# Preloaded late rows put in column order blocks ahead, the last scatter repeated behind the join, the flag read at step nine of every late block

## The chip, the cores and the metric

The kernel runs on one core of a Trainium2 chip. The metric is the device time of one execution in microseconds. PE is TensorE (matmuls), DVE is VectorE, ACT is ScalarE, POOL is GpSimd, SP is SyncE, which here only issues DMAs. PEld is PE's weight load, which runs beside its matmuls. A q behind an engine's name (PEq, POOLq) is its sequencer.

## The reference: what is computed

Three layers stand one behind the other. Eight batches of 3072 positions with 256 values pass a layer in the frequency domain, then 24576 tokens a two-layer network of width 2048, then a mixture of eight experts with room for 768 tokens each:

```python
X = rfft(x, axis=1)
Yr, Yi = Xr @ w_r - Xi @ w_i + b_r, Xr @ w_i + Xi @ w_r + b_i
Y = sign(.) * max(abs(.) - 0.01, 0)             # both parts
x = irfft(Y, n=3072, axis=1).reshape(24576, 256)

h = max(x @ w_in, 0); x = (h * h) @ w_out       # 256 -> 2048 -> 256

logits = x @ w_gate; e = argmax(logits)
# token i, in order: kept while its expert has fewer than 768 tokens so far
disp[e, counts[e]] = x[i]; pos[i] = counts[e]; counts[e] += 1
y = max(disp @ w1, 0) @ w2                      # per expert, 256 -> 1024 -> 256
out[i] = prob[i, e] * y[e, pos[i]]  if kept, else 0
```

Tokens that come after their expert is full give zeros. With this data all eight experts are full after about two thirds of the tokens.

## The kernel before

**Blocks and steps.** The 24576 tokens are worked in 48 blocks of 512, six to a batch; `b, o = divmod(i, 6)`. A block has 16 steps f; step f makes 128 of the 2048 hidden values (`l1`, six matmuls on PE, three products that split the number into a high and a low part). Blocks 0 to 10 are full: `l2` follows in each step, and `route` sends their rows into `disp`, the experts' input. Blocks from 11 on are *late*: from the hidden values only the gate's logits are made (`l2_gate`, at step 10 for the first half and at step 2 of the next block for the rest), since most of their tokens find their expert full. `route(i - 1)` then works beside block i, as a list of small operations (`rops`), of which so many are issued per step: 8 where `steps` is empty, else 5. `steps` are the operations of the next batch's FFT; they are empty at o = 0, o = 1 and, from about step 7, at o = 5.

**What route does in a late block.** DVE finds the chosen expert of each token (`oh`), PE counts by a prefix product with a triangular matrix (`prefix`, L652 and L654), DVE makes the places `pos`, the mask of the kept tokens `kp`, the new counts, the `flag` (some expert still has room), a second prefix product over `kp` gives each kept token's rank (`lp`, `li`). Four scatters on POOL (L667, `late<-zm,li`) write the weight, the token's number and its slot into the table `late`, by rank. `lcnt` and `nlate` count the late rows.

**The nested branches.** From block 12 on each block has one step, FX, at which all remaining small operations are issued and every engine reads the flag (L1227) and branches; the rest of the program stands inside that branch. FX is 9, or 7 (`FX_BARE`) where `steps` is empty. When no expert has room any more, the program leaves through the Else of that block to a common join. In this data it leaves at block 31 (b = 5, o = 1). In an Else (L1144) each engine only brings its semaphores to where the other way would have brought them; POOL waits there for its scatters.

**Behind the join.** The kept late tokens are computed again, with the whole network, in chunks of 256 rows: `late_rows` loads 256 entries of `late` (SP) and gathers the rows by token number from the DRAM array `yr` (POOL, two gathers); `row_order` copies them into column order (by halves of the 256 columns instead of bands of 32); `redo_y` transposes them on PE and splits them; `redo` runs the 16 steps and scatters into `disp`. Chunk c + 1 is loaded at step 4 of chunk c, put in order at step 5 and transposed at step 13. Seven chunks run here. The first chunk's rows, `row0`, are loaded and gathered already in step 1 of every block with o = 0 from block 12 on (12, 18, 24, 30), but put in order behind the join, one half by DVE and one by POOL. There SP also loads the first expert's weights (`m2_loadw(0)`, two loads of 1 MB) ahead of chunk 1's rows. The experts' phase follows.

**Transposes of the block's own rows.** At step 8 (`y_rows`) DVE turns the block's input rows and SP writes them to `yr`. At o = 5, step 9, the FFT stage's loads `xc<-z` are issued by SP, and PE uses them in the steps behind it (L417).

The lists are worked in this order within a step: `l1`, the scatters (`moves`, up to four a step), the small operations, `row0`, `y_rows`, the FFT, the flag.

Of the kernel before, what the change touches and what calls it, by code (L numbers as in the profile page):

```python
# [8 lines left out]
F32 = mybir.dt.float32  # L9
F32R = mybir.dt.float32r  # L10
BF16 = mybir.dt.bfloat16
I32 = mybir.dt.int32
# [7 lines left out]
P = 128  # L20
# [7 lines left out]
def fft_mix__moe__moe2_kernel(  # L28
# [20 lines left out]
    nc = tc.nc  # L49
    NB, S, D = x.shape  # L50
# [11 lines left out]
    TPB = BLK // P  # L62
    MW = 3
# [5 lines left out]
    RB = min(BLK, 256)  # L69
    NREDO = -(-NSLOT // RB)  # L70
    NSURE = max(NFULL + 1, -(-NSLOT // BLK))
# [22 lines left out]
    LG_WAIT = 0  # L94
    LG_T = 4
    PER_F = 5
    PER_BARE = 8
    FX_BARE = 7
    WARM = 16
    Y_F = 8  # L100
    assert E <= CG and KF == 2 * GQ and GQ % 4 == 0 and FX < GF
# [11 lines left out]
    yr = dram1.tile([NTOK, D], F32, name="yr")  # L113

    idt = keep.tile([P, P], F32, name="idt")
    zero = keep.tile([P, D], F32, name="zero")

    f1 = big.tile([N1, N1], F32, name="f1")
    gm = big.tile([N1, N1], F32, name="gm")
# [16 lines left out]

    flag = big.tile([P, 1], I32, name="flag")
    npre = big.tile([P, 1], I32, name="npre")

    class Fft:  # L140
        pass
# [467 lines left out]
    def by_half(ap):  # L609
        return ap.rearrange("p (k b c) -> p k b c", k=2, c=Q)  # L610

    def by_band(ap):
        return ap.rearrange("p (b k c) -> p k b c", k=2, c=Q)
# [49 lines left out]
    def scatter(dst, n, idx, zt, later=None, tiles=TPB):  # L663
# [15 lines left out]
        for t in range(tiles):  # L679
            if later is None:  # L680
                one_tile(t)
            else:
                later.append(lambda t=t: one_tile(t))

    def route(i, zt, lg, lt):
        v = nc.vector
        ops = []
# [65 lines left out]
        if lt is not None:  # L753
            lp = small([TPB + 1], F32, "lp")
            lx = small([TPB], F32, "lx")
            li = W.li()

            def ranks():
                pv = prefix(kp5.unsqueeze(2), 1)
                v.tensor_scalar(lp, pv[:, :, 0], lcnt, None, op0=ALU.add)  # L760

            ops.append(ranks)
            op(
                v.scalar_tensor_tensor,
                lx, lp[:, 0:TPB], -float(BIG), kp5[:, 0:TPB], op0=ALU.add, op1=ALU.mult,
            )
            op(v.tensor_scalar, li, lx, float(BIG), None, op0=ALU.add)
            last.append(lambda: v.tensor_copy(lcnt, lp[:, TPB:]))
            last.append(lambda: v.tensor_copy(nlate, lp[:, TPB:]))  # L769
            dst, n, idx = late, NREDO * RB, lambda t: li[:, t:t + 1]  # L770
        else:
            dst, n, idx = disp, NSLOT, lambda t: zt[:, t, D + 2:D + 3]
# [88 lines left out]
                oob_is_err=False,  # L861
            )

    def row_order(lt, rows, engs=(gp, gp)):
        for t in range(RB // P):
            engs[t % 2].tensor_copy(by_half(lt[:, t * D:(t + 1) * D]), by_band(rows[:, t, 0:D]))
        return lt

    def buf_init():
# [17 lines left out]
    def zero_fill():  # L887
        return [
            lambda r=r, buf=buf: nc.sync.dma_start(
                out=buf[r:r + ZR, :].rearrange("(p k) d -> p k d", p=P),  # L890
                in_=zero.unsqueeze(1).to_broadcast([P, ZR // P, D]),
            )
            for buf in (yr, out) for r in range(0, NTOK, ZR)
        ]
# [86 lines left out]
    with tc.manual_schedule():  # L981
# [150 lines left out]

        def go_on(value):
            guard = tc.If(value)
            ifs.append((guard, guard.__enter__()))

        def warm(p):
            for _ in range(WARM):
                nc.tensor.matmul(p[:, 0:D], idt, zero)

        def close_ifs(other=None):
            while ifs:
                guard, here = ifs.pop()
                guard.__exit__(None, None, None)  # L1144
                if other:
                    with here.Else():
                        other()

        for i in range(NBLK):
            b, o = divmod(i, BPB)  # L1150
# [22 lines left out]
            for f in range(KF):  # L1173
                hook = None
                if i + 1 < NBLK:
                    if f == (KF - 3 if o + 1 < BPB else KF - 1):
                        split_y(i + 1, 0)
                    if f == KF - 1:
                        hook = lambda i=i: split_y(i + 1, 1)
                q.append(l1(ys[i], f, not full, hook=hook, bare=not steps))  # L1180
                if i == 0 and f < 3:
                    combine_w(f)
                if f == CARRY and carry:
                    l2_gate(acc, GQ, carry)
                    pend = evac_gate(acc, *pend)
                if f == (CARRY if carry else 1) and pend is not None:
                    rops = route(i - 1, *pend)
                for _ in range(1 if full else MV):
                    if moves:
                        moves.pop(0)()  # L1190
                for _ in range(3 if full else PER_F if steps else PER_BARE):
                    if rops:
                        step = rops.pop(0)
                        if step is None:
                            break
                        step()
                if f == 1 and o == 0 and i >= NSURE:
                    nc.gpsimd.tensor_copy(npre, nlate)
                    late_rows(0, row0)

                if not full and f == Y_F:
                    y_out = y_rows(i)
                if y_out and f > Y_F:
                    y_out.pop(0)()
                if full and f >= 2:
                    l2(acc, f - 2, q)
                if f not in SKIP[full] or o == BPB - 1:
                    fft_share(1)
                if o == BPB - 1 and b + 1 < NB:
                    if f == SB_F:  # L1210
                        fft(1000)
                        for c in range(3):
                            load_z(st, c)
                        last = sb_steps(st)
                    if f >= KF - 1 - len(SB_N) and f < KF - 1:
                        for _ in range(SB_N[f - KF + 1]):
                            last.pop(0)()
                if not full and f == GF:
                    l2_gate(acc, 0, q)
                if f == (FX if steps else FX_BARE) and i >= NSURE:  # L1220
                    while moves or rops:
                        step = (moves or rops).pop(0)
                        if step is not None:
                            step()
                    if pair[0]:
                        fft(1)
                    rv = nc.values_load(flag[0:1, 0:1], min_val=0, max_val=1)  # L1227
                    go_on(rv > 0)
                if i < NSURE:
                    left = KF * (min(NSURE, NFULL, NBLK) - i) - f  # L1230
                    for k, n in ((0, KF - f), (1, left)):
                        for _ in range(-(-len(fill[k]) // max(n, 1))):
                            fill[k].pop(0)()
# [17 lines left out]
        while moves or rops:  # L1251
            step = (moves or rops).pop(0)
            if step is not None:
                step()
        close_ifs()
        spare.update({0: [], 1: []})
        CT = cap // P
        KD = F2 // P
# [15 lines left out]
        if NBLK > NFULL:  # L1274
# [44 lines left out]
                scatter(disp, NSLOT, lambda t: rows[:, t, D + 2:D + 3], rows, tiles=RT)  # L1319
                return (nxt, y_nxt) if ahead else None  # L1320

            nxt = row0, redo_y(row_order(W.lt(), row0, (ve, gp)))
            nv = nc.values_load(nlate[0:1, 0:1], min_val=0, max_val=NREDO * RB)
            n0 = nc.values_load(npre[0:1, 0:1], min_val=0, max_val=NREDO * RB)
            w_t[0] = m2_loadw(0)
# [220 lines left out]
```

## Time and profile before

| | |
|---|---|
| median of 3 runs | 2073.98 us (2072.65 to 2074.11) |
| the profiled execution | 2076.15 us, span 2074.4 us |
| mean granted clock of PE | 0.983 |
| PE busy | 1996.4 us (96%) |
| DVE, ACT, POOL busy | 1112.8 (54%), 1029.1 (50%), 465.9 us (22%) |
| POOL's scatters `late<-zm,li` | 80, 83.9 us, 1049 ns each |
| DMA | 231.06 MB, mean 111 GB/s |

The shares are of the span. Of the 40 slices of the span PE is busy 9 tenths or more in all but three: the first, the one with the join of the branches (from 1608 us) and the one with the start of the experts' phase (from 1763 us). The granted clock is below 9 tenths of full speed in the same three.

### The profile page before, as it was taken

What the parts mean: (1) busy time and instruction counts of PE and PEld (TensorE: products, weight loads), DVE (VectorE), ACT (ScalarE), POOL (GpSimd) and SP (SyncE); (2) the same over time, 40 slices, a digit from 0 to 9 for tenths busy, and PEclk for the clock granted to TensorE, in tenths of its full rate; (3) what the DMA queues carried; (4) which work ended last, traced back from release to release, by engine and by line L of the source; (5) the groups of instructions that cost most, each with busy time, mean ns of one, the idle gap of its engine ahead of it and who ended that gap; (6) DMA issues with size and microseconds to landing.
All of it is one profiled execution on the core that took longest, in us unless ns stands there. A gap on an engine that the chain in (4) does not pass through costs nothing. (4 is left out here: it accounts for less than half of the span.)

```text
span 2074.4 us, 33524 instructions
## 1 busy us (share of the span) xinstructions
PE 1996.4 (96%) x12577; PEld 1699.4 (82%) x12577; DVE 1112.8 (54%) x2378; ACT 1029.1 (50%) x2051; POOL 465.9 (22%) x495
## 2 busy tenths in 40 slices
PE   6999999999999999999999999999999699799999
PEld 3878999998899898667776687767777699799999
DVE  4846676664566774426634366334653466545352
ACT  3654444444444444566545665466554355424241
POOL 3730111110011111102211122201221122145442
PEclk8999999999999999999999999999999899899999
DMA  8769765567511113162332532333332100643400
GB/s 264 227 193 160 233 208 168 193 202 218 168 31 53 52 37 92 21 166 71 85 93 45 149 84 79 87 83 109 101 88 55 49 27 22 155 120 95 123 16 31
DMA packets 254271, 231.06 MB, mean 111 GB/s; under 512 B 97695, under 2 KB 230544, under 8 KB 254082
## 3 DMA queue, kind: packets, MB, share of 16 engines
q1 hardware_dynamic: 238322, 188.14, 33.0%
q0 software_dynamic: 10384, 21.63, 3.3%
q10 hardware_dynamic: 5376, 18.88, 2.6%
q8 instruction: 105, 1.72, 0.3%
q14 instruction: 84, 0.69, 0.1%
HBM read 111.40 MB, written 118.85 MB: 111 GB/s over the span
## 5 line engine op out<-in xcount | busy, mean ns | idle before, releaser
L549 PE MATMUL ph<-yh,wi_s 128*128 128x512 f32 (+1 forms) x1776 | 499.8, 403 | 6.3 <-DVE sf L691 3.7
L549 PEld LDWEIGHTS ph<-yh,wi_s 128*128 128x128 f32 x1776 | 311.3, 190 | 93.6 <-issue 21.7
L580 PE MATMUL acc<-wo_s,sh 128*128 128x264 f32 (+1 forms) x1792 | 337.4, 284 | 0.0
L580 PEld LDWEIGHTS acc<-wo_s,sh 128*128 128x128 f32 x1792 | 286.8, 188 | 13.6
L571 DVE TENSOR_TENSOR s<-s 128x512 f32<-128x512 f32 (+1 forms) x272 | 170.5, 627 | 202.0 <-ACT sh L570 195.8
L549 PE MATMUL ph<-yl,wi_s 128*128 128x512 f32 (+1 forms) x888 | 269.5, 385 | 0.2
L580 PE MATMUL acc<-wo_s,sl 128*128 128x264 f32 (+1 forms) x896 | 254.7, 284 | 1.0 <-DVE sl L572 1.0
L386 POOL TENSOR_TENSOR xc<-ue 64x256 f32<-64x256 f32 x120 | 101.0, 842 | 636.3 <-DVE ue L381 420.0
L567 ACT ACTIVATE s<-ph 128x512 f32<-128x512 f32 (+1 forms) x224 | 123.0, 549 | 229.5 <-PE ph L549 225.9
L560 ACT ACTIVATE ls<-ph 128x512 f32<-128x512 f32 x220 | 130.7, 594 | 175.2 <-PE ph L549 164.5
L549 PEld LDWEIGHTS ph<-yl,wi_s 128*128 128x128 f32 x888 | 163.1, 189 | 34.9 <-DVE yl L538 1.5
L572 DVE TENSOR_TENSOR sl<-s,sh 128x512 fp32r<-128x512 f32 (+1 forms) x272 | 163.0, 599 | 20.6 <-PE acc L549 0.5
L580 PEld LDWEIGHTS acc<-wo_s,sl 128*128 128x128 f32 x896 | 168.6, 188 | 1.9 <-DVE sl L572 1.9
L549 PE MATMUL acc<-yh,wi_s 128*128 128x512 f32 (+1 forms) x624 | 158.6, 376 | 2.2 <-DVE sf L691 1.9
L564 ACT ACTIVATE ls<-ls 128x512 f32<-128x512 f32 x248 | 156.6, 631 | 7.8
L667 POOL DMA_INDIRECT late<-zm,li x80 | 83.9, 1049 | 320.1 <-DVE nlate L769 131.6
L570 ACT ACTIVATE sh<-s 128x512 fp32r<-128x512 f32 (+1 forms) x272 | 151.4, 557 | 8.7
L1438 ACT ACTIVATE rh<-pg 128x384 fp32r<-128x384 f32 x128 | 62.6, 489 | 161.3 <-PE pg L1429 161.3
L1453 PE MATMUL po<-w2s,rh 128*128 128x256 f32 x768 | 138.5, 283 | 0.0
L1429 PE MATMUL pg<-xh,w1s 128*128 128x384 f32 x512 | 133.5, 339 | 3.6 <-issue 3.0
L549 PEld LDWEIGHTS acc<-yh,wi_s 128*128 128x128 f32 x624 | 104.8, 190 | 31.1 <-issue 8.5
L562 DVE TENSOR_TENSOR ls<-ls 128x512 f32<-128x512 f32 x80 | 55.4, 693 | 129.8 <-ACT ls L560 118.7
(301 smaller groups left out, 3430.2 us busy)
## 6 DMA issues: line engine op xcount, KB each, us to landing
yr<-zero SPq DMA_DIRECT2D x48, 512.0 KB
out_dram<-zero SPq DMA_DIRECT2D x48, 512.0 KB
uj<-u SPq DMA_DIRECT2D x72, 256.0 KB
z<-ue SPq DMA_DIRECT2D x72, 256.0 KB
xc<-z SPq DMA_DIRECT2D x46, 384.0 KB
u<-ue ACTq DMA_DIRECT2D x43, 384.0 KB
xc<-in_x_dram SPq DMA_DIRECT2D x35, 384.0 KB
yr<-zt SPq DMA_DIRECT2D x80, 128.0 KB
```

Of the source, the lines that this page charges most:

```text
L386: y_eng[n == r].tensor_tensor(y[64 * r:64 * r + 64, :], t[src, r, :], c[src, r, :], op=ALU.subtract)
L549: nc.tensor.matmul(p, wi_s[:, l, k, f * P:(f + 1) * P], y[:, k, 0:n_tok], start=(n == 0), stop=(n == 5),)
L560: nc.scalar.activation(s, p, AF.Relu)
L564: nc.scalar.activation(s, s, AF.Square)
L567: nc.scalar.activation(s, p, AF.Relu)
L570: nc.scalar.activation(sh, s, AF.Square)
L571: nc.vector.tensor_tensor(s, s, s, op=ALU.mult)
L572: nc.vector.tensor_tensor(sl, s, sh.bitcast(F32), op=ALU.subtract)
L580: nc.tensor.matmul(acc[t][:, 0:width], a[:, t * P:(t + 1) * P], wo_s[:, m, f, 0:width], start=(f == 0 and n == 0), stop=(f == KF - 1 and n ...
L667: inst = nc.gpsimd.indirect_dma_start(out=dst[:, :], out_offset=bass.IndirectOffsetOnAxis(ap=idx(t).bitcast(U32), axis=0), in_=zt[:, t, :] ...
L1429: nc.tensor.matmul(p[:, 0:gs], w1s[:, l, k, f * P:(f + 1) * P], y[:, k, g * gs:(g + 1) * gs], start=(n == 0), stop=(n == 5),)
L1453: nc.tensor.matmul(acc, a[:, t * P:(t + 1) * P], w2s[:, m, f, :], start=(n == 0), stop=(n == 3 * KD - 1),)
```

## The change

Five things are edited. (1) `PER_BARE` and `FX_BARE` go: five small operations a step and the flag at step 9 in every late block. (2) `row_order(zero, row0)` follows the gathers of `row0` in step 1 of the blocks 12, 18, 24 and 30, both halves on POOL; it writes into `zero`, a tile which is widened from 256 to 512 columns and whose zeros are needed only at the program's start. Behind the join `redo_y(zero)` transposes from there. (3) At the flag only `rops` is emptied, no longer `moves`. (4) Each Else, and the end of the last block, copies the last block's indices and entries (`li`, `zm`) to `lif` and `zmf` with three DVE copies (`hold`). (5) Behind the join four scatters write `zmf` by `lif` into `late`.

```diff
--- before.py
+++ after.py
@@ -94,8 +94,6 @@
     LG_WAIT = 0
     LG_T = 4
     PER_F = 5
-    PER_BARE = 8
-    FX_BARE = 7
     WARM = 16
     Y_F = 8
     assert E <= CG and KF == 2 * GQ and GQ % 4 == 0 and FX < GF
@@ -113,7 +111,7 @@
     yr = dram1.tile([NTOK, D], F32, name="yr")
 
     idt = keep.tile([P, P], F32, name="idt")
-    zero = keep.tile([P, D], F32, name="zero")
+    zero = keep.tile([P, RB // P * D], F32, name="zero")
 
     f1 = big.tile([N1, N1], F32, name="f1")
     gm = big.tile([N1, N1], F32, name="gm")
@@ -136,6 +134,8 @@
 
     flag = big.tile([P, 1], I32, name="flag")
     npre = big.tile([P, 1], I32, name="npre")
+    lif = big.tile([P, TPB], I32, name="lif")
+    zmf = big.tile([P, TPB, MW], F32, name="zmf")
 
     class Fft:
         pass
@@ -682,6 +682,8 @@
             else:
                 later.append(lambda t=t: one_tile(t))
 
+    held = []
+
     def route(i, zt, lg, lt):
         v = nc.vector
         ops = []
@@ -754,6 +756,7 @@
             lp = small([TPB + 1], F32, "lp")
             lx = small([TPB], F32, "lx")
             li = W.li()
+            held[:] = [li, zt]
 
             def ranks():
                 pv = prefix(kp5.unsqueeze(2), 1)
@@ -861,9 +864,9 @@
                 oob_is_err=False,
             )
 
-    def row_order(lt, rows, engs=(gp, gp)):
+    def row_order(lt, rows):
         for t in range(RB // P):
-            engs[t % 2].tensor_copy(by_half(lt[:, t * D:(t + 1) * D]), by_band(rows[:, t, 0:D]))
+            nc.gpsimd.tensor_copy(by_half(lt[:, t * D:(t + 1) * D]), by_band(rows[:, t, 0:D]))
         return lt
 
     def buf_init():
@@ -888,7 +891,7 @@
         return [
             lambda r=r, buf=buf: nc.sync.dma_start(
                 out=buf[r:r + ZR, :].rearrange("(p k) d -> p k d", p=P),
-                in_=zero.unsqueeze(1).to_broadcast([P, ZR // P, D]),
+                in_=zero[:, 0:D].unsqueeze(1).to_broadcast([P, ZR // P, D]),
             )
             for buf in (yr, out) for r in range(0, NTOK, ZR)
         ]
@@ -1132,19 +1135,25 @@
 
         def go_on(value):
             guard = tc.If(value)
-            ifs.append((guard, guard.__enter__()))
+            ifs.append((guard, guard.__enter__(), list(held)))
 
         def warm(p):
             for _ in range(WARM):
-                nc.tensor.matmul(p[:, 0:D], idt, zero)
+                nc.tensor.matmul(p[:, 0:D], idt, zero[:, 0:D])
 
         def close_ifs(other=None):
             while ifs:
-                guard, here = ifs.pop()
+                guard, here, block = ifs.pop()
                 guard.__exit__(None, None, None)
                 if other:
                     with here.Else():
-                        other()
+                        other(block)
+
+        def hold(block):
+            li, zm = block
+            nc.vector.tensor_copy(lif, li)
+            nc.vector.tensor_copy(zmf[:, :, 0:1], zm[:, :, 0:1])
+            nc.vector.tensor_copy(zmf[:, :, 1:].bitcast(I32), zm[:, :, 1:].bitcast(I32))
 
         for i in range(NBLK):
             b, o = divmod(i, BPB)
@@ -1188,7 +1197,7 @@
                 for _ in range(1 if full else MV):
                     if moves:
                         moves.pop(0)()
-                for _ in range(3 if full else PER_F if steps else PER_BARE):
+                for _ in range(3 if full else PER_F):
                     if rops:
                         step = rops.pop(0)
                         if step is None:
@@ -1197,6 +1206,7 @@
                 if f == 1 and o == 0 and i >= NSURE:
                     nc.gpsimd.tensor_copy(npre, nlate)
                     late_rows(0, row0)
+                    row_order(zero, row0)
 
                 if not full and f == Y_F:
                     y_out = y_rows(i)
@@ -1217,9 +1227,9 @@
                             last.pop(0)()
                 if not full and f == GF:
                     l2_gate(acc, 0, q)
-                if f == (FX if steps else FX_BARE) and i >= NSURE:
-                    while moves or rops:
-                        step = (moves or rops).pop(0)
+                if f == FX and i >= NSURE:
+                    while rops:
+                        step = rops.pop(0)
                         if step is not None:
                             step()
                     if pair[0]:
@@ -1252,7 +1262,9 @@
             step = (moves or rops).pop(0)
             if step is not None:
                 step()
-        close_ifs()
+        hold(held)
+        close_ifs(hold)
+        scatter(late, NREDO * RB, lambda t: lif[:, t:t + 1], zmf)
         spare.update({0: [], 1: []})
         CT = cap // P
         KD = F2 // P
@@ -1319,7 +1331,7 @@
                 scatter(disp, NSLOT, lambda t: rows[:, t, D + 2:D + 3], rows, tiles=RT)
                 return (nxt, y_nxt) if ahead else None
 
-            nxt = row0, redo_y(row_order(W.lt(), row0, (ve, gp)))
+            nxt = row0, redo_y(zero)
             nv = nc.values_load(nlate[0:1, 0:1], min_val=0, max_val=NREDO * RB)
             n0 = nc.values_load(npre[0:1, 0:1], min_val=0, max_val=NREDO * RB)
             w_t[0] = m2_loadw(0)
```

What stands on POOL in the last two blocks that run, 30 and 31, before (`row_1535` is `row0`, `zm` and `li` the entries and indices of a block's late rows):

```order
L1198 COPY npre<-nlate 128x1
L853 DMA row_1535<-yr,row_1535 128x256 x2
L691 IOTA zm_1528 128x4
L667 DMA late<-zm_1528,li_1533 6144x3 x4
L1227 TENSOR_LOAD flag
L1144 COMPARE_AND_BRANCH
L691 IOTA zm_1529 128x4
L667 DMA late<-zm_1529,li_1534 6144x3 x4
L1227 TENSOR_LOAD flag
L1144 COMPARE_AND_BRANCH
```

And the same place of the changed kernel (`row_1537` is `row0`):

```order
L1207 COPY npre<-nlate 128x1
L856 DMA row_1537<-yr,row_1537 128x256 x2
L869 COPY zero<-row_1537 128x256 x2
L693 IOTA zm_1530 128x4
L667 DMA late<-zm_1530,li_1535 6144x3 x4
L1237 TENSOR_LOAD flag
L1147 COMPARE_AND_BRANCH
L693 IOTA zm_1531 128x4
L667 DMA late<-zm_1531,li_1536 6144x3 x4
L1237 TENSOR_LOAD flag
L1147 COMPARE_AND_BRANCH
```

The two copies into `zero` have come behind the gathers of block 30. The four scatters of each block stand ahead of its flag read, as before: the scatters are among the moves that are issued at the start of step 9.

POOL at the join before, up to the end of chunk 0 (`zt_1527` holds the rows of chunk 1):

```order
L1144 UNCONDITIONAL_BRANCH
L866 COPY lt_1532<-row_1535 128x256
L1323 TENSOR_LOAD nlate
L1324 TENSOR_LOAD npre
L1144 COMPARE_AND_BRANCH
L853 DMA zt_1527<-yr,zt_1527 128x256 x2
L866 COPY lt_1532<-zt_1527 128x256 x2
L667 DMA disp<-row_1535 6144x259 x2
```

And in the changed kernel:

```order
L1147 UNCONDITIONAL_BRANCH
L667 DMA late<-zmf,lif 6144x3 x4
L1335 TENSOR_LOAD nlate
L1336 TENSOR_LOAD npre
L1147 COMPARE_AND_BRANCH
L856 DMA zt_1529<-yr,zt_1529 128x256 x2
L869 COPY lt_1534<-zt_1529 128x256 x2
L667 DMA disp<-row_1537 6144x259 x2
```

The copy has gone, and in its place four scatters stand ahead of the gathers of chunk 1.

DVE at the end of block 31's routing before (`ls` is the gate's hidden values, `zt` the transposed rows of the block):

```order
L691 TENSOR_SCALAR li_1534<-lx 128x4
L768 COPY lcnt<-lp 128x1
L769 CAST nlate<-lp 128x1
L562 TENSOR_TENSOR ls_8138<-ls_8138 128x512
L1227 TENSOR_LOAD flag
L1144 COMPARE_AND_BRANCH
L623 STREAM_TRANSPOSE zt_1526<-yT 128x1024
```

And in the changed kernel:

```order
L693 TENSOR_SCALAR li_1536<-lx 128x4
L771 COPY lcnt<-lp 128x1
L623 STREAM_TRANSPOSE zt_1528<-yT 128x1024
L562 TENSOR_TENSOR ls_8142<-ls_8142 128x512
L772 CAST nlate<-lp 128x1
L1237 TENSOR_LOAD flag
L1147 COMPARE_AND_BRANCH
```

The transpose now precedes the flag read, and SP's first write of the transposed rows to `yr` with it.

## Rows read from the trace of the kernel before

**Rows 1.** Waits of PE, 780 to 1616 us: total, times, longest.
```profile
PE ph L549 <- DVE sf L691: 3.7, 2, 1.9
PE acc L652 <- DVE kp L691: 1.4, 4, 0.3
PE acc L417 <- DMA xc<-z: 0.6, 1, 0.6
```

**Rows 2.** Chain of waits, 1600 to 1660 us: start, duration, what.
```profile
1599.91 1.41 PE ph L549 x6
...
1625.96 5.79 issue
1632.29 0.41 POOL lt L866
...
1633.89 1.66 PE ph L549 x6
```

**Rows 3.** Timeline at the exit, the join and chunk 1: start, us, engine, [idle before].
```profile
1616.70 1.48 POOL L667 DMA_INDIRECT late<-zm,li  x1 [22.21 <-DVE nlate L769]
...
1621.07 0.98 POOL L667 DMA_INDIRECT late<-zm,li  x1 [0.30 <-issue]
...
1623.44 1.19 SPq L1270 DMA_DIRECT2D yT<-in_moe_w_dram  x1
...
1626.54 0.45 PE L1295 MATMUL px<-idt,lt 128*128 128x128 f32 x1 [10.58 <-DVE lt L866]
...
1634.28 1.06 POOL L853 DMA_INDIRECT zt<-yr,zt  x1 [1.59 <-DVE yl L478]
...
1638.63 0.40 POOL L866 COPY lt<-zt 128x256 f32<-128x256 f32 x1 [0.89 <-DMA zt<-yr,zt]
...
1653.01 0.60 PE L1295 MATMUL px<-idt,lt 128*128 128x128 f32 x4
```

**Rows 4.** Instructions of line 1144 around the exit: ns min/median/max, first and last start.
```profile
L1144 POOLq EVENT_SEMAPHORE  x6: 17/30/43, 1622.2 to 1622.7; - x6
L1144 PEldq COMPARE_BRANCH  x2: 3085/3293/3501, 1615.1 to 1619.0; - x2
...
L1144 DVEq EVENT_SEMAPHORE  x2: 21/21/21, 1620.0 to 1620.1; - x2
...
L1144 POOLq INC_SWDGE_SEM  x1: 1050/1050/1050, 1624.8 to 1624.8; - x1
L1144 POOLq COMPARE_BRANCH  x1: 46/46/46, 1625.9 to 1625.9; - x1
```

**Rows 5.** Instructions of line 409, blocks 17 and 23.
```profile
L409 SPq EVENT_SEMAPHORE  x4: 17/28/28, 1053.0 to 1058.0; - x4
...
L409 SPq EVENT_SEMAPHORE  x4: 17/22/28, 1300.1 to 1304.7; - x4
```

**Rows 6.** Timeline of blocks 17 and 23, DVE and PE.
```profile
1051.37 1.25 DVE L623 STREAM_TRANSPOSE zt<-yT 128x1024 f32<-128x1024 f32 x1 [0.37 <-issue]
...
1059.45 0.80 PE L417 MATMUL acc<-gm,xc 96*128 96x96 f32 x6
...
1305.06 0.69 PE L417 MATMUL px<-gm,xc 96*128 96x96 f32 x5
```

**Rows 7.** Stretches: us, busy by engine PE to POOL, PEclk, DMA share, GB/s.
```profile
1633.90:1638.50 4.60, 4.60 (x22) 4.60 (x23) 2.21 (x6) 2.12 (x6) 2.48 (x3) 0.51 0.20 57
...
1781.00:1786.00 5.00, 5.00 (x14) 4.09 (x15) 0.00 (x0) 0.42 (x1) 0.00 (x0) 0.58 0.02 7
...
1051.30:1054.70 3.40, 3.40 (x10) 2.63 (x9) 1.25 (x1) 1.23 (x2) 2.11 (x3) 0.50 0.31 57
```

**Rows 8.** Timeline of a later chunk's rows: load, first gather, second copy.
```profile
1687.01 0.36 SPq L848 DMA_DIRECT2D zt<-late  x1
...
1689.50 1.05 POOL L853 DMA_INDIRECT zt<-yr,zt  x1 [4.25 <-DMA zt<-late]
...
1694.68 0.61 POOL L866 COPY lt<-zt 128x256 f32<-128x256 f32 x1 [1.71 <-DMA zt<-yr,zt]
```

## The prediction

> **What bounds the kernel now.** I read the table of PE's waits first, over the stretch of the late blocks, then the chain of waits around the join, then the timeline there, then the clock by stretches. PE is the bound nearly everywhere, so what the change can be worth is the sum of PE's gaps that it touches; work on other engines beside a busy PE costs nothing. The waits show three kinds of gap in the late blocks. Three times PE stops 1.9 us for the flag read that stands behind step 7, in blocks 17, 23 and 29 (the row on ph holds two of them; the third, of the same size, fell on acc). Eight times it stops 0.35 us for the kept mask (1.4 us on acc for four, and four more of that size on px): the blocks 12, 13, 18, 19, 24, 25, 30 and 31. Once, in block 29, it waits 0.6 us for an FFT load [rows 1]. The largest gap lies behind the exit of block 31. The reader is to see there that PE is idle 10.58 us to its first transpose at 1626.54, and that it then waits again, because POOL's copy of the second half of the preloaded rows starts at 1632.29 only, after 5.79 us of "issue"; step 0 of the first late chunk starts at 1633.89 [rows 2, 3]. The instructions of the branches say why POOL comes last: it has waited for its scatters (the semaphore instruction at 1624.8, 1.05 us), branches at 1625.9 and then shows nothing until 1631.75. Two branches of PE took 3.1 and 3.5 us [rows 4].
>
> **Flag back to step nine, five operations a step.** Blocks 14 to 16, 20 to 22 and 26 to 28 already work so and show no such gap, so I remove the gaps of the others. *Mask:* seven blocks other than 31 lose 0.35 us each: −2.45. *Blocks 17, 23, 29:* 3 x 1.85 = 5.6 us of gap go, but next in line is the load xc<-z. Its landing is the last event of line 409, 1058.0 in block 17 and 1304.7 in block 23 [rows 5]; PE used it at 1059.45 and 1305.06 [rows 6], and in block 29 right as it landed, since it waited for it [rows 1]. The load stands on SP behind the first write of the transposed rows, and that behind DVE's transpose, which now comes ahead of the branch; by its 0.37 us of idle there and 0.07 for the one small operation passed, it starts about 0.45 us earlier [rows 6]. So the gaps can shrink by 1.85 (1.45 + 0.45 covers it), 0.36 + 0.45 = 0.8, and 0.45: −3.1. What remains is a gap in front of the FFT stage, and gaps can cost clock: after the 1.85 us gap in block 17 the granted clock was 0.50 (the lower of the two levels) over 3.4 us, which costs 1.7 [rows 7]. I take 0.8 back for one half of such a drop: −2.3. Bounds: 0 (all given back), and −5.6 − 1.7 = −7.3 with the drop in block 17 gone and every load early.
>
> **Row order ahead of the join.** Two POOL copies of 0.40 us [rows 3] and the wait for the two gathers are added to blocks 12, 18, 24 and 30. Behind them on POOL stand the iota and the four scatters of that block, which nobody waits for on PE; POOL is idle over 20 us before such scatters (22.21) [rows 3]. Cost 0; if that cover were gone, 0.8 us a block plus the gathers' landing. The DVE copy and the POOL copy behind the join go.
>
> **The exit.** The changed kernel leaves two steps later and without the mask's gap: 2 x 1.41 − 0.35 = +2.47 [rows 1, 2]. POOL's Else began at 1622.2 [rows 4]; now at about 1624.7, and this is the last thing that PE needs for its transposes, since these read rows put in order long ago. From the copy's start at 1632.29 over three transposes and the split to step 0 it was 1.6 [rows 2]; the copy's 0.41 goes and a fourth transpose, 0.45 [rows 3], comes: 1.6 again. Step 0 starts at 1626.3 instead of 1633.89: −7.6. The three small DVE copies of the hold (4 to 8 values a partition) are hidden: DVE's Else began at 1620.0, 2.2 us before POOL's [rows 4].
>
> **The new wait.** The order shows that the four scatters in front of the flag have stayed, and four more of the same rows stand behind the join: the last scatter is doubled, not moved. Behind them on POOL are the two gathers of chunk 1; SP's load of the chunk's rows reads the table that they write, so it waits until the last has landed. Step by step: semaphore instruction at 1624.8 + 2.5 = 1627.3, branch at 1628.4. The branch took 5.8 us before, and this is the term that I know least. Lower bound 3.1 (PE's). Upper bound: the first weight load is issued on SP behind a write that now precedes the flag, so I put the loads some 3.9 us later than 1623.44 rather than 2.5; if POOL comes back only behind them, it is 1631.75 + 3.9 = 1635.7, or a microsecond more. I take 5.8 + 0.4, as it is nearest to the one row of this very branch: 1634.6. Then 0.5 to the first scatter as to the copy at 1632.29; four scatters at 0.98 with 0.30 between (the first 1.48 beside a DVE operation [rows 3]): last one from 1639.0; landed 3.8 after its start (1621.07 to 1624.8): 1642.8. From the load's issue to the first gather 2.5, from there to the end of the second copy 5.2 + 0.6 [rows 8], or 4.8 as in chunk 0 (1634.28 to 1639.03) [rows 3]: 1650.1 to 1651.1, I take 1650.4. Chunk 1's transposes came at 1653.01, 19.1 us behind step 0 [rows 2, 3], so PE wants them at 1645.4: a stall of 5.0 us. From then on the kernel is ahead by 7.6 − 5.0 = 2.6. Behind a stall of that size the clock falls, by the row at the start of the experts' phase, 0.58 over 5 us [rows 7]: 42% of 5 = 2.1 lost. The half clock behind the exit (0.51 over 4.6 us) stays in both. Net of the join −0.5, with bounds −7.6 (no stall) and +2 (POOL back 2.5 us later still).
>
> A rule of the Trainium skill speaks to this branch. The page "Runtime: NRT & Kernel Launch", section "Instruction fetch mechanics", says that a taken branch whose target is outside the pages held forces a DMA fetch before the engine can go on. PE's 3.1 and 3.5 us and POOL's 5.8 agree that far. Nothing in the sum rests on it.
>
> **Sum.** −2.45 − 2.3 − 0.5 = −5.2 on the profiled execution's 2076.15, which is 2.2 above the median of the runs shown; the same difference from the median 2073.98 gives **2068.8**. About 0.2%, 4.1 us, is what a measurement of this kernel can tell from no change, so the bounds of "same" are 2069.8 and 2078.1. The likeliest case's own range is 2065.5 to 2072.
>
> **Rivals.** *POOL returns early.* Its 5.8 us before lay beside two weight loads (the later issued at 1623.44 for 1.19 us [rows 3]), while PE's branches without such traffic took 3.1 to 3.5. If the fetch isn't held behind the loads, or leaves before them, POOL is back at 1628.4 + 3.3 = 1631.7, all behind it 2.9 earlier, the stall 2.1 and perhaps no drop of the clock: 2.9 + 2.1 better, 2063.8. For it: the branch is now only about 1 us behind the loads, it was 2.5 behind. Against: the loads still come first. In the Trainium skill, "DMA: Bandwidth & Descriptors", section "Queues, rings and completion order", says that each DMA engine takes turns between the queues it has work for, packet by packet. That would let a small fetch through the weight loads; the 5.8 us of before speak against it, since the fetch then would hardly have waited. It gives no other time than this rival's.
>
> *The gaps in the middle don't pay.* Each of the three late blocks waits for its FFT load anyway (block 29 does already), a new gap there drops the clock, and only the mask's 2.45 and the join's 0.5 stay: 2071 to 2073, no change. For it: block 29's wait. Against: two of the three had time to spare.
>
> *The doubled scatter sets the end (slower).* Mechanism: POOL's second scatter, load and gathers of chunk 1 are one chain of 16 us behind POOL's return (1634.6 to 1650.4). PE's gain is gone when the stall and the clock behind it reach 7.6 + 4.75 = 12.4, a stall of 10.3, which is POOL back at 1639.9. It is slower by 0.2% from about 1644 on: 4.1 us more, 2078 and up. Price at that return: 2078 to 2081. For it: nothing starts on POOL for 5.8 us in the trace, and a chain with three DMAs has spread. Against: it would take a branch of 15 us. The same end comes nearer if the exit's Else, now with work of DVE and its waits in it, is longer than I count: each microsecond of it costs one.
>
> *The change doesn't do what it says.* The doubling is this already, and is in the sum. Had the first four been gone, POOL would be free some 5 us sooner and the stall zero: 2073.98 − 2.45 − 2.3 − 7.6 = 2061.6. The order excludes it.
>
> **How the numbers follow.** Forecast 0.45, of which two thirds lie under 2069.8 and the rest within 0.2%; early POOL 0.20, all faster; no pay in the middle 0.21, nearly all the same; slower chain 0.12, of which 0.11 past the bound; other small mixtures 0.02. Faster 0.30 + 0.20 + 0.02 = 0.52, same 0.15 + 0.21 + 0.01 = 0.37, slower 0.11. The range for 8 in 10 reaches from 2062 (the early POOL and a little more) to 2075 (the middle case, with a little of the chain).
>
> **What would show it.** In the waits after: no flag wait of 1.9 us, no mask wait of 0.3; a wait of PE for xc<-z of up to 2 us in blocks 23 and 29, none in 17. Behind the exit: PE's gap some 8 us, step 0 eight microseconds earlier by the old clock, POOL's four scatters after an issue of 6 us, and then a gap of about 5 us on PE in front of the transposes of chunk 1, waiting for POOL's copy lt, with a granted clock near 0.5 behind it. I am wrong if that gap is missing (then faster), if it exceeds 10 us (then slower), or if gaps appear in the blocks at step 9 itself. All else, the full blocks and the experts' phase, should keep its time.

## The result and the profile after

The changed kernel took 2050.45 us (median of 4 runs, 2048.20 to 2055.34) against 2073.32 (2071.00 to 2074.11): a ratio of 0.9895 with a 95% interval of 0.9873 to 0.9917, 22.9 us faster. Measured again later it was 0.9877 [0.9852, 0.9901]. Forecast were 2068.8 and a range from 2062: the direction was right, the size was short by 18 us, and the time lies outside the range. The profiled execution of the changed kernel took 2052.55 us, span 2050.5.

Where the 23.9 us between the two spans went is read by equal work: the times of the same product of PE in both traces are laid beside each other. At the start of block 12 the changed kernel is 1.0 us ahead, behind the mask of block 30 14.7, at step 0 of the first late chunk 23.4, at the end 23.9. So 13.7 us come from the late blocks up to there and 8.7 from the rest of blocks 30 and 31 and the join. The 1.0 at block 12 hides two numbers: the setup took 2.6 longer (it took 154.6 to 161.0 us in the traces of all runs), and the full blocks with the start of block 11 took 3.6 less, though the diff doesn't touch the full blocks.

The waits of PE from block 11 on to the first chunk (total, times, longest), after:

```profile
PE px L1307 <- POOLq L1147: 6.1, 1, 6.1
...
PE acc L417 <- DMA xc<-z: 1.6, 3, 0.6
...
PE px L417 <- DMA xc<-z: 0.6, 1, 0.6
```

The waits for the flag and for the mask [rows 1] are gone. In their place stand waits for the FFT load, 2.2 us in all where there was 0.6. The two waits at the join [rows 2, 3] have become one of 6.1 us. The step 0 of chunk 0 in the chain of waits, after:

```profile
1610.51 1.81 PE ph L549 x6
```

It answers to the 1633.89 of [rows 2]. The timeline at the exit and the join, after (lines in order of engine):

```profile
1603.72 0.99 POOL L667 DMA_INDIRECT late<-zm,li  x1 [21.89 <-DVE lcnt L771]
...
1607.59 0.98 POOL L667 DMA_INDIRECT late<-zm,li  x1 [0.30 <-issue]
1609.33 1.09 PE L1307 MATMUL px<-idt,zero 128*128 128x128 f32 x4 [6.09 <-POOLq L1147]
1611.54 0.40 SPq L1281 DMA_DIRECT2D yT<-in_moe_w_dram  x1
1612.06 0.44 SPq L1282 DMA_DIRECT2D yT<-in_moe_w_dram  x1
1614.76 1.03 POOL L667 DMA_INDIRECT late<-zmf,lif  x1 [6.19 <-DVE sl L572]
...
1618.65 0.98 POOL L667 DMA_INDIRECT late<-zmf,lif  x1 [0.30 <-issue]
1620.79 0.88 SPq L851 DMA_DIRECT2D zt<-late  x2
1623.46 1.04 POOL L856 DMA_INDIRECT zt<-yr,zt  x1 [3.83 <-issue]
1627.77 0.41 POOL L869 COPY lt<-zt 128x256 f32<-128x256 f32 x1 [0.96 <-DMA zt<-yr,zt]
1629.19 0.60 PE L1307 MATMUL px<-idt,lt 128*128 128x128 f32 x4
```

And the instructions of the branches (ns min/median/max, first and last start), after, which answer to [rows 4]:

```profile
L1147 POOLq EVENT_SEMAPHORE  x6: 17/30/43, 1609.1 to 1609.7; - x6
...
L1147 POOLq COMPARE_BRANCH  x2: 46/48/50, 1605.7 to 1611.0; - x2
...
L1147 POOLq INC_SWDGE_SEM  x1: 1050/1050/1050, 1609.9 to 1609.9; - x1
```

Read the chain of the forecast against it. PE's last step of block 31 ends at 1603.24 (1609.33 less the 6.09 of idle), 15.2 us earlier than the forecast had it in the times of the old trace; 15.2 added to a time of the changed kernel gives the old time. PE's transposes start as POOL's Else begins (1609.1 and 1609.33): this step was right. The weight loads are issued up to 1612.06, which is 1627.3 in old time: this was right too. But the scatters start earlier behind that end, the first of them takes 0.99 us and not 1.48, and from the last one's start to the semaphore instruction it is 2.3 us (1607.6 to 1609.9), not 3.8. So POOL's branch at 1611.0 stands 2.2 us earlier than in the forecast, and with that ahead of the weight loads and not behind them; its queue works again at 1613.5, 2.5 us later, where 5.8 us passed before, and the first scatter runs at 1614.76. Chunk 1's rows are in order at 1628.2, PE takes them at 1629.2. The stall of 5.0 us isn't there; the room is 1.0 us.

One difference isn't in any wait. The same 600 us of full blocks, before and after (PE busy and its instructions stand first):

```profile
200.00:800.00 600.00, 598.51 (x3889) 538.64 (x3888) 389.58 (x780) 278.90 (x514) 82.63 (x97) 1.00 0.44 138
```
```profile
200.00:800.00 600.00, 598.30 (x3909) 540.17 (x3908) 391.68 (x784) 280.73 (x519) 82.24 (x97) 1.00 0.45 139
```

PE is busy all the time at the full clock in both, and yet it gets 20 instructions (0.5%) further. Between the starts of two successive matmuls of line 549 that read yl it is 233.9 ns on average before and 228.9 after. Such a count moves with the place of the window in the work, so here is the same work by its ends, the first prefix product of the full blocks and the first product with the gate's weights in block 11, before and after:

```profile
228.00 0.20 PE L652 MATMUL px<-oh,tri 128*128 128x40 bf16 x1
...
808.14 1.92 PE L592 MATMUL acc<-ls,wgate 128*32 128x512 f32 x16
```
```profile
230.19 0.19 PE L652 MATMUL px<-oh,tri 128*128 128x40 bf16 x1
...
807.13 1.92 PE L592 MATMUL acc<-ls,wgate 128*32 128x512 f32 x16
```

That is 580.1 us before and 576.9 after.

### The profile page after: what moved, and what is told of

Same layout as the page of the kernel before. It is cut to its first block, busy times and chain, and to the rows that moved or that the text cites. A ratio compares the mean times of both kernels' runs of the same rounds, so it can differ in the third digit from the quotient of the medians.

```text
span 2050.5 us, 33573 instructions
## 1 busy us (share of the span) xinstructions
PE 1988.2 (97%) x12589; PEld 1697.4 (83%) x12589; DVE 1113.1 (54%) x2382; ACT 1032.0 (50%) x2054; POOL 469.3 (23%) x506
## 5 line engine op out<-in xcount | busy, mean ns | idle before, releaser
L667 POOL DMA_INDIRECT late<-zm,li x80 | 78.9, 987 | 308.7 <-DVE lcnt L771 241.4
```

What stands on the lines that cost most here:

```text
L667: inst = nc.gpsimd.indirect_dma_start(out=dst[:, :], out_offset=bass.IndirectOffsetOnAxis(ap=idx(t).bitcast(U32), axis=0), in_=zt[:, t, :] ...
```

## Experiments

All are timed against the kernel before in the same rounds, three of them; intervals are 95%. For the pace I give the mean time between the starts of two successive yl matmuls in the full blocks.

**Does the place of the tiles set the pace?** The change widens `zero` (later tiles move by 1024 bytes a partition) and adds `lif` and `zmf` (96 bytes more). The theory was that the place of yh and yl, the rows that PE streams, sets the pace. e1 and e2 take the two moves singly:

```diff
     npre = big.tile([P, 1], I32, name="npre")
+    pad = big.tile([P, 24], F32, name="pad")        # e1
-    zero = keep.tile([P, D], F32, name="zero")
+    zero = keep.tile([P, RB // P * D], F32, name="zero")   # e2
```

> The kernel before with one unused tile of 96 bytes a partition behind npre, which moves all later tiles (the split input rows yh and yl among them) by 96 bytes, as lif and zmf do in the changed kernel. Nothing else differs. The traces of before and after show PE's 128x512 matmuls of line 549 in the unchanged full blocks at a start-to-start median of 234 ns before and 231 to 232 after. Theory 'placement': this comes from where the tiles lie; full blocks 3 to 4 us shorter, late blocks 3 to 4 us shorter, 2064 to 2067 us in all, with the gaps of before (three of 1.87, eight of 0.35, 10.6 + 5.8 at the join) still there. Rival 'not placement' (the chip, or the order of instructions): 2073 us, 234 ns.

> The kernel before with the tile zero widened to 512 columns and only its first 256 used, which moves all later tiles by 1024 bytes. Theory 'placement by the 96 bytes' (the start of yh stays at 32 modulo 64): no change, 2073 us, 234 ns for a 128x512 matmul. Rival 'placement by the 1024 bytes': 2064 to 2067 us, 231 ns. Rival 'not placement': 2073 us.

e1: 2067.69 us, 0.9951 [0.9936, 0.9966], pace 229.3. e2: 2075.22, 0.9992 [0.9977, 1.0007], pace 233.9. So 96 unused bytes make the kernel some 10 us faster, and 1024 nothing. The same stretch of e1:

```profile
200.00:800.00 600.00, 598.34 (x3903) 540.34 (x3902) 389.77 (x780) 281.17 (x520) 84.76 (x100) 1.00 0.44 138
```

e3 and e4 look from the other side: the changed kernel without the doubled scatter, its copies and its two tiles, at the tiles' places of e2 and of the changed kernel.

```diff
-        hold(held)
-        close_ifs(hold)
-        scatter(late, NREDO * RB, lambda t: lif[:, t:t + 1], zmf)
+        close_ifs()
+    pad = big.tile([P, 24], F32, name="pad")        # e4 only
```

> The changed kernel without the four scatters behind the join, without the three DVE copies of the hold and without the tiles lif and zmf; so its tiles lie as in e2. Theory 'placement by the 96 bytes, doubled scatter hidden': gaps as in the changed kernel, 6.1 us at the join, no stall ahead of chunk 1, but 234 ns per matmul: 2073.3 - 10 (gaps in the blocks) - 7.9 (join) = 2055 to 2058 us. Rival 'doubled scatter costs time': faster than the changed kernel's 2050.5. Rival 'not placement': 2050 us.

> e3 with the unused tile of 96 bytes, so that its tiles lie as in the changed kernel, without the doubled scatter. Theory 'placement, doubled scatter hidden': the same as the changed kernel, 2048 to 2052 us, 231 to 232 ns, and 7 to 9 us less than e3. Rival 'doubled scatter costs time': 2 us or more below the changed kernel. Rival 'not placement': the same as e3.

e3: 2061.18, 0.9932 [0.9906, 0.9957]. e4: 2050.43, 0.9875 [0.9856, 0.9895], the changed kernel's time. So the doubled scatter costs nothing that intervals of 4 us would show, and the place is worth about as much with the other edits as without. e3 came out 3 us above its range, which was reckoned from 2073.3 for the kernel before; that took 2077.15 in these rounds. By the ratio the other edits gave 14 us, not the 15 to 18 of the range.

e5 and e6 ask for the rule, by 32 and 64 bytes in the place of 96 (`pad` of 8 and 16 columns):

> The kernel before with an unused tile of 32 bytes a partition behind npre. It moves the later tiles by 32 bytes, so yh and yl start at a multiple of 64 bytes, as they do with 96. Theory 'the start modulo 64': as with 96 bytes, 0.4 to 0.6% below before, and some 3900 PE instructions between 200 and 800 us where before has 3889. Rival 'the distance moved, or a larger modulus such as 128 (the start is 64 modulo 128 here, 0 with 96 bytes)': no change.

> The same with 64 bytes: yh and yl start at 32 modulo 64, as before. Theory 'the start modulo 64': no change against before, 3889 PE instructions between 200 and 800 us. Rival 'any move helps, or a larger modulus': up to 0.5% below before.

The theory of 64 bytes fell, in both runs: e5, which it had faster, was 2074.54, 0.9995 [0.9982, 1.0008], pace 233.8; e6, which it had unchanged, was 2069.34, 0.9973 [0.9956, 0.9990], pace 232.4. e9 moves yh and yl by 96 bytes, e10 all behind them by 96, e14 moves yh and yl by 224, e11 is e3 with yh and yl moved as in e9. What stands behind yh and yl moves as well, by 128 bytes in e9 and e11 and by 256 in e14:

```diff
+        pad0 = lb.tile([P, 24], F32, name="pad0")   # e9, e11; 56 columns in e14
         W.yh = Ring("yh", [P, 2, BLK], F32R, 2, lb)
         W.yl = Ring("yl", [P, 2, BLK], F32R, 1, lb)
+        pad1 = lb.tile([P, 8], F32, name="pad1")    # e10: 24 columns here, no pad0
```

> The kernel before with an unused tile of 96 bytes ahead of yh and one of 32 bytes behind yl: only yh and yl move by 96 bytes, to a start at a multiple of 128, what follows them moves by 128 and keeps its place modulo 128, what stands ahead stays. So far the mean start-to-start of the yl matmuls in the full blocks was 229 ns in all runs with yh and yl at a multiple of 128 bytes, and 232 to 234 at 32, 64 and 96. Theory 'yh and yl at a multiple of 128 bytes': 229 ns, 0.4 to 0.5% below before (some 2066). Rival 'another of the tiles that moved (FFT tiles ahead, ls or sh behind)': 234 ns, no change.

> The kernel before with the unused tile of 96 bytes behind yl: yh and yl stay at 32 modulo 128, all behind them (zt, ls, s, sh, sl) moves by 96. Theory 'yh and yl': no change but for the late chunks, 234 ns. Rival 'the tiles behind': 0.4 to 0.5% below before.

> The kernel before with an unused tile of 224 bytes ahead of yh and one of 32 bytes behind yl: yh at 172544, a multiple of 256 as well as of 128; all else keeps its place modulo 128. Theory 'a multiple of 128': as e9, 229 ns for the yl matmuls and 0.35% below before. Rival 'it must be 128 modulo 256': no change, 234 ns.

> e3 (the changed kernel without the doubled scatter) with yh and yl alone moved to a multiple of 128 bytes as in e9. Theory 'yh and yl': the blocks as fast as in the changed kernel, the late chunks as fast as in before (118 ns instead of 119 to 120 for their yh matmuls, some 1 us): 2048 to 2050 us, the lowest of all. Rival 'other tiles': as e3, 2061 us.

e9: 2068.77, 0.9965 [0.9954, 0.9977], pace 229.5. e10: 2075.88, 0.9994 [0.9981, 1.0007], pace 233.3. e14: 2071.88, 0.9984 [0.9971, 0.9997], pace 233.1. e11: 2055.72, 0.9903 [0.9883, 0.9923], pace 229.5. For the pace of the yl matmuls it is yh and yl, by e9 against e10, unless the 128 bytes behind them did it in e9; no run parts the two. That a multiple of 128 bytes is enough for this pace fell with e14: it was below 230 at all starts at 128 modulo 256 (reckoned from e14's expectation, which puts yh at 172544), and 232.4 to 233.9 at 0, 32, 64 and 96.

But the yl matmuls aren't the whole of it. The work between the two products shown above took:

| start of yh modulo 256 | run | pace, ns | us |
|---|---|---|---|
| 32 | before (e2, e3, e7, e8 and e13 alike) | 233.9 | 580.1 |
| 32, all behind moved by 96 | e10 | 233.3 | 580.0 |
| 64 | e5 | 233.8 | 578.5 |
| 96 | e6 | 232.4 | 577.9 |
| 128, yh, yl and all behind moved | e9 | 229.5 | 577.9 |
| 128, all later tiles moved | e1 (changed kernel, e4 alike) | 229.3 | 577.0 |
| 0 | e14 | 233.1 | 578.8 |

The kernels whose tiles lie alike agree within 0.2 us. e9 has 2.3 of e1's 3.1 us, and e6 has 2.2 of them at nearly the old pace. So the place of other tiles counts too, and which ones, and by what rule, is open.

e11 was not the lowest of all, as I had expected: its late chunks weren't faster, and the rest of the difference from e4 lies at the edge of the intervals.

**What are the parts worth alone?**

```diff
-    PER_BARE = 8
-    FX_BARE = 7
+    PER_BARE = 5                                    # e7
+    FX_BARE = 9                                     # e7
                     late_rows(0, row0)
+                    row_order(zero, row0)           # e8, with zero widened
-            nxt = row0, redo_y(row_order(W.lt(), row0, (ve, gp)))
+            nxt = row0, redo_y(zero)                # e8
```

> The kernel before with the flag at step 9 and five operations a step in every late block, and nothing else (rows put in order behind the join as before, tiles lying as before). Read from the traces of before and after: the gaps in the blocks shrink by 5.6 (three flag reads with what follows them, less the waits for the FFT load) and 4.4 (mask); the program leaves two steps later, and POOL's copy at the join still comes after its branch, so the join costs 2.2 more than before. Theory 'parts add': 7 to 9 us below before. Rival of the prediction (gaps given back at the FFT load and by the clock): 2 to 4 us below.

> The kernel before with the rows of chunk 0 put in order in blocks 12, 18, 24 and 30 and transposed from the tile zero, widened to 512 columns as in e2; flag, operations per step and scatters as before. Theory 'POOL's Else is the last thing that PE needs': step 0 of chunk 0 comes 7 to 8 us earlier, chunk 1's rows are wanted 7 to 8 us earlier too and are still in time, 7 to 8 us below before. Rival 'chunk 1's rows are late then': a stall of 2 to 5 us ahead of its transposes, 3 to 5 us below before.

e7: 2069.22, 0.9969 [0.9951, 0.9987], some 6 us, between its theory (7 to 9) and its rival (2 to 4). e8: 2066.72, 0.9958 [0.9944, 0.9971]. e8 shows the join as forecast without a stall: one wait of 6.4 us, and none ahead of chunk 1. In e7's profile PE ran into the FFT load in block 17 and lost the clock, which the forecast had priced as a bound. The wait in the timeline, and the two stretches behind it (the granted clock is the third number from the end):

```profile
1061.19 1.13 PE L417 MATMUL acc<-gm,xc 96*128 96x96 f32 x8 [2.44 <-DMA xc<-z]
```
```profile
1061.00:1066.00 5.00, 4.81 (x28) 4.81 (x29) 0.56 (x1) 0.98 (x2) 0.00 (x0) 0.66 0.71 141
1066.00:1072.00 6.00, 6.00 (x35) 5.44 (x34) 1.12 (x2) 1.60 (x3) 0.00 (x0) 0.71 0.51 131
```

By the clock alone these 11 us cost 3.4. In the profile of the changed kernel the same wait was 0.65 us and the clock stayed; in e16, the same kernel once more, two waits of 0.51 and 0.41 stood there and the clock fell behind them:

```profile
1054.00:1061.00 7.00, 7.00 (x30) 6.42 (x29) 0.56 (x1) 1.72 (x3) 0.00 (x0) 0.51 0.63 159
```

So this term is not the same from run to run. By equal work over the blocks 17, 23 and 29 the gain was 5.3 us in the changed kernel, 2.2 in e16 and none (−0.2) in e7.

**Is the room at chunk 1 really 1 us, and does the scatter's chain set it?** e12 writes the scatter behind the join twice.

```diff
         scatter(late, NREDO * RB, lambda t: lif[:, t:t + 1], zmf)
+        scatter(late, NREDO * RB, lambda t: lif[:, t:t + 1], zmf)
```

> The changed kernel with its scatter behind the join written twice (eight scatters). In the changed kernel chunk 1's rows were ready at 1628.2 and wanted at 1629.2, with POOL's chain of scatters, load and gathers ahead of them. Four more scatters are 5.1 us, with a wait for the first four to land perhaps 6 to 7. Theory 'the chain is as the prediction has it, only with 1 us of room': a stall of 4 to 6 us of PE ahead of chunk 1's transposes, with a lower clock behind it, 4 to 8 us above the changed kernel. Rival 'something else sets when the rows come (the load of the weights, SP)': no stall, no change.

2060.36 us, 0.9928 [0.9910, 0.9946], some 8 to 10 us above the changed kernel of other rounds, where 4 to 8 were expected. In the trace the stretch from step 0 of the first late chunk to the experts' first product is 7.6 us longer than in the changed kernel. Its waits show the stall of the forecast, and a lower clock in that stretch:

```profile
PE px L1308 <- POOL lt L869: 4.9, 2, 4.0
```
```profile
1629.00:1634.00 5.00, 3.78 (x18) 3.59 (x19) 0.85 (x2) 0.78 (x3) 0.59 (x2) 0.66 0.08 22
```

So the mechanism of the forecast's new wait is there; in the changed kernel it ends a microsecond before it would count.

**Why was POOL back early?** The eighteen traces fall into two groups of nine. From POOL's branch to its next instruction behind the join it took 5.2 to 5.8 us where SP had issued the first weight load 2.4 to 3.6 us ahead of the branch (the kernel before, e1, e2, e5, e6, e8, e9, e10, e14), and 2.5 to 2.7 where SP issued it 0.4 to 1.5 behind (the changed kernel, e3, e4, e7, e11, e12, e13, e15, e16). e13 is the test: only the place of the loads is changed.

```diff
                             nxt = redo_load(c + 1)
+                            if c == 0:
+                                w_t[0] = m2_loadw(0)
...
-            w_t[0] = m2_loadw(0)
```

> The kernel before with the first expert's two weight loads issued on SP behind the load of chunk 1's rows instead of ahead of it; nothing else. Theory 'the loads hold POOL's fetch and landings': the weights are then issued behind POOL's branch; the branch takes 2.5 to 3.3 us instead of 5.8, PE's second wait at the join shrinks from 5.75 to some 3 us, perhaps the landing of the scatters comes 1 us earlier too: 2.5 to 4 us below before. Rival 'the branch takes its time whatever the DMA queues do': no change.

2071.45 us, 0.9977 [0.9966, 0.9987], 4.8 us below before. The chain of waits and the timeline of e13:

```profile
1623.68 2.67 issue
1626.89 0.41 POOL lt L866
1627.34 0.49 PE px L1295
```
```profile
1618.71 0.98 POOL L667 DMA_INDIRECT late<-zm,li  x1 [0.30 <-issue]
1623.91 0.39 SPq L848 DMA_DIRECT2D zt<-late  x1
...
1624.74 0.39 SPq L1269 DMA_DIRECT2D yT<-in_moe_w_dram  x1
...
1627.34 0.90 PE L1295 MATMUL px<-idt,lt 128*128 128x128 f32 x3 [2.64 <-POOL lt L866]
```

The 5.79 us of issue [rows 2] are 2.67: two 1 MB loads issued ahead of POOL's branch hold its return by 3 us. I had weighed the rule of the Trainium skill, "DMA: Bandwidth & Descriptors", section "Queues, rings and completion order", that a DMA engine takes turns between its queues, packet by packet. By that rule a small fetch would have passed the loads; that it is a fetch that waits here, no row shows.

The landing of the scatters stayed slow in e13 (1618.7 to 1622.5), so that part of POOL's early return isn't due to the loads. It comes with the flag at step nine: from the last scatter's start to the semaphore instruction it was 2.3 to 2.5 us in all eight traces with it. In e7, where nothing else differs, it was 2.4, the first scatter took 1.00 us, and the branch (1626.49) came ahead of the loads (1627.08). With the flag at step seven it was 3.2 to 4.2 us, but for 2.3 in e5, and the first scatter took 1.47 or 1.48. By what means stays open. The rows of e7:

```profile
1619.15 1.00 POOL L667 DMA_INDIRECT late<-zm,li  x1 [22.36 <-DVE lcnt L768]
...
1623.02 0.98 POOL L667 DMA_INDIRECT late<-zm,li  x1 [0.30 <-issue]
...
1627.08 0.41 SPq L1269 DMA_DIRECT2D yT<-in_moe_w_dram  x1
```
```profile
L1144 POOLq INC_SWDGE_SEM  x1: 1050/1050/1050, 1625.4 to 1625.4; - x1
```

**Is there more to be had?** e15 puts e13's edit into e4; e16 is the changed kernel once more.

> e4 (the changed kernel without the doubled scatter, tiles as in the changed kernel) with the weight loads behind the load of chunk 1's rows, as in e13. POOL's branch was 2.5 us already in the changed kernel, and chunk 1's rows were in time. Theory: no change against the changed kernel, 2048 to 2052. Rival 'the loads still cost at the join': 2 us or more below it.

> The changed kernel once more, beside e15 on the same chip: 2048 to 2055 us, 1.0% below before.

e15: 2051.61, 0.9873 [0.9850, 0.9896]. e16: 2052.20, 0.9877 [0.9852, 0.9901]. No difference: the loads cost nothing once they come behind POOL's branch. No version tried is clearly below the changed kernel.

## Why the prediction was wrong

- *Row order ahead of the join, and the exit:* right. POOL's Else is the last that PE waits for, and step 0 came 8.7 us earlier in the changed kernel by equal work from block 30 on (forecast 7.6 with the two steps and the mask). Alone it measured 8.7 (e8).
- *The new wait:* this step failed. It priced a stall of 5.0 us and 2.1 us of clock; measured were none. The term that failed in it is "semaphore instruction at 1624.8 + 2.5 = 1627.3, branch at 1628.4": POOL came there 2.2 us earlier, overtook the weight loads, and so "5.8 + 0.4" for the branch became 2.5. These 2.2 and 3.7 us are the whole stall and the room of 1 us. The flag at step nine alone brings both (e7). The first rival had the mechanism ("or leaves before them"), at 0.20. The order of the loads and POOL's branch was what counted, as e13 shows.
- *The gaps in the late blocks:* the mechanism was right. In e3 and e7, whose tiles lie as before, the mask cost 0.49 us a block by equal work, not 0.35, and the flag read 2.0 us, not 1.85; the wait costs more than PE's idle time, and by what means isn't shown. That makes 3.4 in seven blocks, for my 2.45. The three blocks with the flag read gave 5.3 in the changed kernel, for my 2.3, but 2.2 in e16: the difference is the clock behind the waits for the FFT load, and that the first profile had no drop there was luck. e7, with a wait of 2.44 us and a lost clock, shows my lower bound of 0. What then lacks to 13.7 in the late blocks is some 5.0, the pace.
- *What no step held:* the place of the tiles, 0.35 to 0.49% or 7 to 10 us of the 22.9. I had said that the full blocks would keep their time; they became 3.6 us shorter. The diff shows the two new tiles and the wider one, and I had taken their cost as none without a reason. e1 and e4 show that 96 bytes of them make the gain.
- *The sum:* from my −5.2 to the −23.9 of the spans it is 18.7 us: 7.1 for the stall and its clock, some 8.6 for the place (3.6 and 5.0), 4.0 for the gaps, 1.1 for the exit, 0.5 behind step 0, less 2.6 for the longer setup. The direction was right, but the largest single item isn't in the prediction at all.
- *The doubled scatter as the slower rival:* its mechanism is real (e12), its point was not reached.

The parts measured alone add up: e1 −0.49%, e7 −0.31% and e8 −0.42% (each within 0.13 to 0.18) make −1.22%; measured were −1.05% and −1.23%.

## What to carry to other kernels

A diff that adds a tile moves every tile allocated behind it; compare the time of an unchanged stretch by equal work before crediting the rest of the edit. A term that is read as "old time plus a shift" holds only if all engines are shifted alike: where two queues race (a branch of one engine, a bulk load of another), price both orders. Issue bulk loads behind the branches that other engines still have to take (0.23% here, e13).

## What the runs showed of the hardware

- Moving yh and yl by 96 bytes a partition, and what lies behind them by 128, changed the time between the starts of two successive 128x512 matmuls that read yl from 233.9 to 229.5 ns (e9); of those that read yh it was 265.2 and 264.5. By what rule is open: this pace was below 230 only at starts at 128 modulo 256, but e6, at 96, had 2.2 us less of the same 580 us at a pace of 232.4. In the late chunks, with 256 columns, the order was another one: 118.3 ns before, 119.7 after, 117.0 in e5 between the starts of yh matmuls.
- POOL's return from a taken branch took 5.8 us with two loads of 1 MB issued 2.5 and 3.0 us ahead of it, and 2.7 without (before and e13); in all eighteen traces it was 5.2 to 5.8 with the loads ahead and 2.5 to 2.7 with them behind.
- A wait of PE that shows 0.35 us of idle time cost 0.49 us by equal work, and one of 1.87 us cost 2.0 (e3, e7).
